# An mLSTM layer with an MLP on one core: a planner's order replaced by a fixed list, a 128-row third K tile, and the norm factor moved to the residual

## The chip, the cores and the metric

The kernel runs on one NeuronCore of a Trainium2 chip. The number that counts is device time in microseconds (us) of one execution, input layouts prepared beforehand on the host. The profile comes from one further execution of the same program on the chip; its times are in us from the first to the last instruction, which the profile calls the span. Engines carry the profile's names: PE is TensorE, PEld its weight loads, DVE is VectorE, ACT is ScalarE, POOL is GpSimd, SP is SyncE, which here only issues DMAs.

## What is computed

Four batches, 8 heads, 768 time steps, head size 40, all in fp32. First a gated recurrence in every head, then layer norm and a two-layer MLP on the 320 joined features:

```python
for t in range(S):
    m_new = np.maximum(f_gate[:, :, t] + m, i_gate[:, :, t])
    f_stab = np.exp(f_gate[:, :, t] + m - m_new)
    i_stab = np.exp(i_gate[:, :, t] - m_new)
    ...
    C = f_stab * C + i_stab * einsum('bhd,bhe->bhde', vt, kt)
    n = f_stab * n + i_stab * kt
    h_tilde = einsum('bhde,bhe->bhd', C, qt)
    denom = np.maximum(np.abs(einsum('bhd,bhd->bh', n, qt)), 1.0)
    y[:, :, t] = sigmoid(o_gate[:, :, t]) * h_tilde / denom
x  = y with the heads joined                    # (4, 768, 320)
xn = (x - mean(x)) / np.sqrt(var(x) + 1e-06) * g_ln
out = x + np.maximum(xn @ w_ch1, 0.0) @ w_ch2   # 320 -> 1280 -> 320
```

(The shapes of f_stab and i_stab are left out in this copy.)

## The kernel before

**Tiling.** Time is cut into 6 chunks of 128 steps. One chunk of one batch is a *step* `st` (24 of them, chunk by chunk, 4 batches in each); two steps are a *pair* `p` (12), and the MLP of one pair's 256 tokens is a *unit* `u` (12).

**A step.** For each head PE multiplies keys and queries into a 128x128 tile `s` (L411). A matrix `w` of decays comes from the gates: the gate rows of the chunk lie in DRAM (`gsc`), a DMA spreads 8 of them, 512 KB, over 128 partitions (`load_G`, L332), POOL cuts the triangle (`select`, L339), ACT takes 8 exponentials with a bias from `ar_sb` (L363). DVE multiplies `s` into `w` (`emit_P`, L418). PE then forms `Y`: the part from earlier chunks out of the state (`emit_inter`, L432, with queries that POOL has scaled by `eg`, L346) and the part within the chunk (`emit_pv`, L481). There is one buffer `Y`, so `emit_inter` of the next step waits until `Y` has been read. The state is updated from L444, L462 and L470.

**The norm.** DVE takes the denominator and its reciprocal (L496, L502, L507), POOL multiplies it into the output gate (`norm_o`, L514: `ogr`), DVE multiplies `Y` by it (L523: `y`, which frees `Y`). Mean and variance come from ACT in half of the steps and from DVE in the others, the root from POOL (L549 to L553: `rstd`), then DVE writes the normalized row twice (L560, and 64 of its columns again, L563). PE turns it (`emit_T`, L578: `xT`), ACT and DVE split it into a high part `xh` with g_ln as a scale (three instructions, L584) and a low part `xl` (L596).

**A unit.** fp32 precision is reached with fp32r operands in high and low parts. `mm1` (L615) adds 8 matmuls of 256 columns into `h` for each block of 128 hidden features; I call these 8 a *batch*; a unit has 10. The 320 features are two K tiles of 128 rows and a third that holds the last 64 features twice (high part in rows 0 to 63, low part in rows 64 to 127). The low half of w1 meets that third tile in its 64 upper rows alone, a matmul of 64 rows:

```python
ops += [(w1l[:, k, cs], XH[:, k]) for k in range(2)]
ops += [(w1l[0:64, 2, cs], XH[0:64, 2])]
```

ACT takes the relu (`hh`, L619), DVE the low part (`hl`, L625), and `mm2` (L639 to L641) adds 6 matmuls of 320 columns for each half of the tokens. DVE adds the residual `y` (L645), SP stores (L649).

**The start.** Weights arrive as 64-bit integers and are taken apart on the chip: one ACT pass, one max pass, three passes on DVE (L681, L685, L689), a high part from ACT (L712), a low part from DVE or POOL (L717); 11 pieces in all. The first three pairs read queries and keys as fp32 with 40 rows; later ones are split and stacked into 120 rows by 6 DMAs in each step (`stack`, L257). For the first 2 steps PE itself makes the decays (`mask_mm`, `sel_mm`, L378 and L389), and 41 matmuls on zeros (`keep_busy`, L373) stand between the others.

**The order.** A planner (`Plan`) hands out tasks by readiness, by assumed durations and by a table of ranks and offsets; each engine then runs its own list strictly in that order. All loads and stores are issued by SP, in one list, and an entry that waits holds up those behind it. In the planner's table an `mm1` batch stands with 0.87 us.

Of the kernel before, what the change touches and what calls it, by code (L numbers as in the profile page):

```python
# [30 lines left out]

TUNE = dict(
    NN=3, k=5, xt=2, yb=4, wb=4, RA=26.71, RB=21.56, f0=18.16, f1=30.7, fd=0.84, ke='aada', ge='dppppp', ns='aaaaadddddaadddadaaddaad', cx='ddpdpdpdpdp', cl='dpddpdpdpdd', nr=-31.54, pr=-13.12, x2=5.36, kd=-11.22, c0=20.24, GP=2, sp=4.1, cst=0.81, og0=2.6, wl0=3.88, wl1=8.52, nt1=8.16, g2=16.0, wu=9, T0=24.67, SL=22.64, EX=6.21, g1=-7.43, p2=0.83, tok1=15.21, s2=6.94, n2=0.0, n3=26.21, og1=29.93, cv=-6.4, cs=2.76, wl=0.34, ws=2.19
)
# [1006 lines left out]
```

## Time and profile before

| | us |
|---|---|
| median of 3 runs (479.43 to 485.68) | 480.65 |
| span of the profiled execution | 477.9 |
| PE busy in it | 440.4 (92%) |
| DVE, ACT, POOL busy | 230.4, 176.2, 159.5 |

The profiled execution's span is 2.75 us under the median; the times count a little work around the span. "Busy" of PE counts matmuls that overlap as one stretch, so it tells when PE had something in flight, not how densely it worked: for that the distance between the starts of matmuls has to be read. [...]

### The profile page before, as it was taken

What the parts mean: (1) busy time and instruction counts of PE and PEld (TensorE: products, weight loads), DVE (VectorE), ACT (ScalarE), POOL (GpSimd) and SP (SyncE); (2) the same over time, 40 slices, a digit from 0 to 9 for tenths busy, and PEclk for the clock granted to TensorE, in tenths of its full rate; (3) what the DMA queues carried; (4) which work ended last, traced back from release to release, by engine and by line L of the source; (5) the groups of instructions that cost most, each with busy time, mean ns of one, the idle gap of its engine ahead of it and who ended that gap; (6) DMA issues with size and microseconds to landing.
All of it is one profiled execution on the core that took longest, in us unless ns stands there. A gap on an engine that the chain in (4) does not pass through costs nothing.

```text
span 477.9 us, 7347 instructions
## 1 busy us (share of the span) xinstructions
PE 440.4 (92%) x2704; PEld 386.5 (81%) x2706; DVE 230.4 (48%) x524; ACT 176.2 (37%) x438; POOL 159.5 (33%) x195
## 2 busy tenths in 40 slices
PE   8999998999789997699998799988979988999996
PEld 4886787889679886688997698977868977989885
DVE  2475869975164752544545325453463443433321
ACT  3356556751151343414443313244243334222200
POOL 1145449661341560613623433252250522100100
PEclk8555779899979999579999859999997998999999
DMA  8935757637845879425776743686465585000000
GB/s 241 291 103 148 233 148 256 163 93 207 190 124 145 235 206 213 122 80 169 194 198 162 183 126 110 161 237 184 130 194 167 132 259 118 1 0 29 0 29 27
DMA packets 52721, 71.82 MB, mean 150 GB/s; under 512 B 3330, under 2 KB 45862, under 8 KB 52686
## 3 DMA queue, kind: packets, MB, share of 16 engines
q1 hardware_dynamic: 52686, 71.36, 54.1%
q8 instruction: 21, 0.34, 0.3%
q14 instruction: 14, 0.11, 0.1%
HBM read 46.83 MB, written 4.12 MB: 107 GB/s over the span
## 4 chain that ended last, share of the span: by engine, by line
PE 61%; DMA 22%; DVE 7%; SPq 3%; POOL 2%; issue 2%; ACT 2%; POOLq 0%; DVEq 0%; ACTq 0%
PE h L615 25%; DMA w<-gsc 8%; PE Y L481 6%; PE o L639 5%; PE s L411 5%; PE o L641 5%; PE o L640 5%; PE kv L444 2%; DMA og<-in_og_dram 2%; DMA raw<-in_qk_dram 2%; DMA ks<-raw 2%; DMA qs<-hi 2%; DMA qs<-raw 2%; SPq L257 2%; DMA eg<-esc 2%
## 5 line engine op out<-in xcount | busy, mean ns | idle before, releaser
L615 PE MATMUL h<-xh,w1h 128*128 128x256 f32 x360 | 91.2, 312 | 0.0
L615 PE MATMUL h<-xh,w1l 128*128 128x256 f32 x360 | 89.4, 327 | 0.0
L639 PE MATMUL o<-w2h,hh 128*128 128x320 f32 x240 | 83.1, 346 | 6.6 <-ACT hh L619 5.4
L619 ACT ACTIVATE hh<-h 128x512 fp32r<-128x512 f32 x60 | 35.6, 594 | 136.0 <-PE h L615 124.4
L641 PE MATMUL o<-w2h,hl 128*128 128x320 f32 x240 | 77.3, 322 | 0.5 <-DVE hl L625 0.5
L640 PE MATMUL o<-w2l,hh 128*128 128x320 f32 x240 | 76.8, 320 | 0.0
L615 PEld LDWEIGHTS h<-xh,w1l 128*128 128x128 f32 x360 | 62.8, 200 | 16.6 <-issue 2.5
L625 DVE SCALAR_TENSOR_TENSOR hl<-h,hh 128x512 fp32r<-128x512 f32 x60 | 41.2, 687 | 63.0 <-ACT hh L619 62.8
L363 ACT ACTIVATE w<-w,ar_sb 128x128 f32<-128x128 f32 x176 | 55.0, 390 | 33.1 <-POOL w L339 32.9
L615 PEld LDWEIGHTS h<-xh,w1h 128*128 128x128 f32 x360 | 64.3, 204 | 0.6
L615 PE MATMUL h<-xl,w1h 128*128 128x256 f32 x240 | 63.6, 348 | 0.0
L481 PEld LDWEIGHTS Y<-tok,w 128*128 128x128 f32 x384 | 55.4, 216 | 1.5 <-POOL rstd L552 1.1
L481 PE MATMUL Y<-tok,w 128*128 128x42 f32 x384 | 53.9, 293 | 0.6 <-ACT xh L584 0.6
L639 PEld LDWEIGHTS o<-w2h,hh 128*128 128x128 f32 x240 | 48.0, 200 | 7.5 <-ACT hh L619 5.8
L615 PEld LDWEIGHTS h<-xl,w1h 128*128 128x128 f32 x240 | 37.9, 199 | 16.4 <-issue 2.2
L641 PEld LDWEIGHTS o<-w2h,hl 128*128 128x128 f32 x240 | 47.6, 198 | 1.5 <-DVE hl L625 1.5
L418 DVE TENSOR_TENSOR w<-s,w 128x512 f32<-128x512 f32 x48 | 33.0, 688 | 31.4 <-PE s L411 26.5
L640 PEld LDWEIGHTS o<-w2l,hh 128*128 128x128 f32 x240 | 47.8, 199 | 0.0
L411 PE MATMUL s<-qs,ks 120*128 120x128 f32 (+1 forms) x240 | 41.0, 305 | 3.9 <-DMA qs<-raw 2.0
L411 PEld LDWEIGHTS s<-qs,ks 120*128 120x128 f32 (+1 forms) x240 | 36.2, 217 | 8.4 <-issue 7.5
L514 POOL TENSOR_TENSOR ogr<-og,rec 128x320 f32<-128x320 f32 x24 | 18.8, 781 | 65.3 <-DVE rec L507 50.1
L248 POOL TENSOR_TENSOR raw<-raw,hi 120x768 f32<-120x768 f32 x18 | 33.0, 1837 | 14.9 <-ACT hi L243 14.9
(91 smaller groups left out, 518.2 us busy)
## 6 DMA issues: line engine op xcount, KB each, us to landing
w<-gsc SPq DMA_DIRECT2D x22, 512.0 KB
tok<-in_tok_dram SPq DMA_DIRECT2D x12, 698.0 KB
raw<-in_qk_dram SPq DMA_DIRECT2D x9, 720.0 KB
ks<-hi SPq DMA_DIRECT2D x36, 180.0 KB
qs<-hi SPq DMA_DIRECT2D x36, 180.0 KB
out_dram<-y SPq DMA_DIRECT2D x24, 160.0 KB
qn<-in_qn_dram SPq DMA_DIRECT2D x10, 360.0 KB
eg<-esc SPq DMA_DIRECT2D x30, 120.0 KB
```

The source lines that it names most:

```text
L248: nc.gpsimd.tensor_tensor(out=raw[:, :, j], in0=raw[:, :, j], in1=hi[:, :, j], op=ALU.subtract)
L363: nc.scalar.activation(out=w[:, h], in_=w[:, h], func=AF.Exp, bias=ar_sb[:, c, 0, hb:hb + 1])
L411: nc.tensor.matmul(ps[:, hh], ks[:, h], qs[:, h], start=True, stop=True)
L418: nc.vector.tensor_tensor(out=w[:, half * 4:half * 4 + 4], in0=s_t.pop((st, half)), in1=w[:, half * 4:half * 4 + 4], op=ALU.mult)
L481: nc.tensor.matmul(Y[:, h * VA:(h + 1) * VA], w[:, h], tok_t[p][:, j, h * VA:(h + 1) * VA], start=(c == 0), stop=(c == 0 or h == H - 1), s ...
L514: nc.gpsimd.tensor_tensor(out=ogr, in0=og_t[c][:, b].rearrange("p (h d) -> p h d", h=H), in1=rec.to_broadcast([128, H, D]), op=ALU.mult,)
L615: nc.tensor.matmul(ps[:, i], a, x, start=(n == 0), stop=(n == len(ops) - 1))
L619: nc.scalar.activation(out=hh, in_=h1_t[p, f], func=AF.Relu)
L625: nc.vector.scalar_tensor_tensor(out=hl.rearrange("p a t -> p (a t)"), in0=ps.rearrange("p a t -> p (a t)"), scalar=0.0, in1=hh.rearrange( ...
L639: nc.tensor.matmul(ps, hh[:, i, sl], w2h[:, ff], start=(ff in (0, 2 * cut)), stop=False)
L640: nc.tensor.matmul(ps, hh[:, i, sl], w2l[:, ff], start=False, stop=False)
L641: nc.tensor.matmul(ps, hl[:, i, sl], w2h[:, ff], start=False, stop=(ff in (2 * cut - 1, KF - 1)))
```

## The change

The planner, its tables and its dummy matmuls are gone. A list of words, `ORDER`, names every piece of work in its order, and a loop calls them:

```diff
-        plan.run()
+        for word in ORDER.split():
+            name, *at = word.split(".")
+            fn = work.get(name) or work[name + "_"]
+            fn(*map(int, at))
```

No word of it is `fill`, the one piece that would issue dummy matmuls. The pieces themselves differ in these places.

**Third K tile.** The last transpose takes features 192 to 319, so that the last 64 land in rows 64 to 127; the low part overwrites rows 0 to 63. The low half of w1 is copied into both halves of its third tile (a fourth copy `cR`), and all 8 matmuls have 128 rows:

```diff
-        for k in range(3):
+        for k in range(2):
             nc.tensor.transpose(ps[:, k], xn[:, k * 128:(k + 1) * 128], id_sb)
+        nc.tensor.transpose(ps[:, 2], xn[:, DM - 128:DM], id_sb)
...
-        ops = [(w1h[:, k, cs], XH[:, k]) for k in range(2)]
-        ops += [(w1l[:, k, cs], XH[:, k]) for k in range(2)]
-        ops += [(w1l[0:64, 2, cs], XH[0:64, 2])]
+        ops = [(w1h[:, k, cs], XH[:, k]) for k in range(3)]
+        ops += [(w1l[:, k, cs], XH[:, k]) for k in range(3)]
         ops += [(w1h[:, k, cs], XL[:, k]) for k in range(2)]
-        ops += [(w1h[:, 2, cs], XH[:, 2])]
```

**Norm.** `norm_o` on POOL is gone. DVE multiplies gate and `Y` at once (`n2`, frees `Y`), then divides, sums and subtracts the mean (`n3`). The variance is taken by ACT beside the path (`sq`), its root by POOL (`np_`), and it is multiplied in only at the residual (`ob`); g_ln is multiplied into w1 when the weights are taken apart:

```diff
+    def n2(st):
+        Y = Y_t.pop(st).rearrange("p (h d) -> p h d", d=VA)
...
+        nc.vector.scalar_tensor_tensor(
+            out=y_t[st].rearrange("p (h d) -> p h d", h=H), in0=og_t[p][:, j].rearrange("p (h d) -> p h d", h=H),
+            scalar=1.0, in1=Y[:, :, 0:D], op0=ALU.add, op1=ALU.mult,
+        )
...
+        nc.vector.reciprocal(out=t1, in_=t1)
+        nc.vector.scalar_tensor_tensor(
+            out=y, in0=y, scalar=1.0, in1=t1.to_broadcast([128, H, D]), op0=ALU.mult, op1=ALU.mult, accum_out=sm
+        )
+        nc.vector.tensor_scalar(out=sm, in0=sm, scalar1=-1.0 / DM, scalar2=None, op0=ALU.mult)
+        xn = xn_p.tile([128, DM], F32, tag="xn", name="xn")
+        nc.vector.tensor_scalar(out=xn, in0=y_t[st], scalar1=sm, scalar2=None, op0=ALU.add)
...
+    def sq(st):
...
+        nc.scalar.activation(out=og_t[p][:, j], in_=xn_t[st], func=AF.Square, accum_out=rs)
...
+        nc.scalar.activation(out=XH_t[p][:, :, j * C:(j + 1) * C], in_=xp_t[st], func=AF.Copy)
...
+            out=y_t[st], in0=m2_t[j], scalar=rs_t.pop(st), in1=y_t[st], op0=ALU.mult, op1=ALU.add
```

**Gate rows.** They lie batch first in DRAM, so that the 8 rows of a step are one run of 4 KB instead of 8 of 512 bytes:

```diff
+            out=w.rearrange("p h t -> p (h t)"),
+            in_=gsc[c].rearrange("(b h) t -> b (h t)", b=B)[b:b + 1].to_broadcast([128, H * C]),
```

The scaled rows `esc` are stored by 5 DMAs in each chunk instead of 2.

**Chunk 0.** All 4 of its steps take their decays from PE (2 before), with `gc` as an operand of 128 rows, zero below row 31; 20 DMAs spread gate rows instead of 22. Only two pairs read fp32 queries and keys, so 20 steps are stacked instead of 18. The gate tile is three half-chunk buffers, `y` has 5 buffers (4), and the low half of w1 comes from DVE always.

**How the lists move.** PE, at a batch of `mm1` in the middle of the program (`h` is its target), before:

```order
L615 MATMUL h<-xh,w1h 128x256 x2
L615 MATMUL h<-xh,w1l 128x256 x3
L615 MATMUL h<-xl,w1h 128x256 x2
L615 MATMUL h<-xh,w1h 128x256
L411 MATMUL s<-qs,ks 128x128 x4
```

and now:

```order
L579 MATMUL h<-xh,w1h 128x256 x3
L579 MATMUL h<-xh,w1l 128x256 x3
L579 MATMUL h<-xl,w1h 128x256 x2
L544 MATMUL xT<-id_sb,xn 128x128 x2
L545 MATMUL xT<-id_sb,xn 128x128
```

The 8 matmuls are the same in number, 3, 3 and 2 instead of 2, 3, 2 and 1; the third `w1l` matmul has 128 rows of operands now, and 64 before.

POOL, over a stretch of about four steps in the middle of the program, before (`ogr` is `norm_o`, `rstd` the root, `qn` scaled queries, `w` the decays, `kp` scaled keys, `raw` low parts of the split):

```order
L339 AFFINE_SELECT w<-w 128x1024
L346 TENSOR_TENSOR qn<-qn,eg 120x3x128
L514 TENSOR_TENSOR ogr<-og,rec 128x320
L346 TENSOR_TENSOR qn<-qn,eg 120x3x128
L339 AFFINE_SELECT w<-w 128x1024
L549 TENSOR_SCALAR rstd<-mv 128x1
L550 TENSOR_TENSOR rstd<-rstd,mh_sb 128x1
L248 TENSOR_TENSOR raw<-raw,hi 120x2x384 x2
L514 TENSOR_TENSOR ogr<-og,rec 128x320
L352 TENSOR_TENSOR kp_140<-tok,ar_sb 128x320
L352 TENSOR_TENSOR kp_141<-tok,ar_sb 128x320
L339 AFFINE_SELECT w<-w 128x1024
```

and now (`rs` is the root):

```order
L415 TENSOR_TENSOR kp_137<-tok,ar_sb 128x320
L352 TENSOR_TENSOR raw<-raw,hi 120x2x384 x2
L532 TENSOR_SCALAR rs<-rs 128x1
L533 TENSOR_TENSOR rs<-rs,mh_sb 128x1
L357 AFFINE_SELECT w<-w 128x1024
L532 TENSOR_SCALAR rs<-rs 128x1
L533 TENSOR_TENSOR rs<-rs,mh_sb 128x1
L357 AFFINE_SELECT w<-w 128x1024
L415 TENSOR_TENSOR kp_138<-tok,ar_sb 128x320
L415 TENSOR_TENSOR kp_137<-tok,ar_sb 128x320
L415 TENSOR_TENSOR kp_138<-tok,ar_sb 128x320
```

`ogr` is gone, and `rs` is read only at the residual; `w`, `raw`, `kp` and `qn` still stand in one list.

SP, at the stores of one unit in the middle of the program (`raw` are queries and keys of a later pair, `w` the decays, `eg` the scaled rows), before:

```order
L649 DMA out_dram<-y 128x320
L297 DMA gsc<-gc_148 32x128
L303 DMA esc<-gg_146 32x128
L304 DMA esc<-gg_146 4x128
L211 DMA raw<-in_qk_dram 120x1536
L221 DMA qn<-in_qn_dram 120x768
L324 DMA eg<-esc 120x1x256 x3
L649 DMA out_dram<-y 128x320
L332 DMA w<-gsc 128x8x128
```

and now:

```order
L196 DMA raw<-in_qk_dram 120x1536
L620 DMA out_dram<-y 128x320
L208 DMA qn<-in_qn_dram 120x768
L255 DMA eg<-esc 120x1x256 x3
L620 DMA out_dram<-y 128x320
L243 DMA w<-gsc 128x1024
```

The two stores stand among the loads as before, the next decays behind the second one.

## Rows read from the trace of the kernel before

**Rows 1.** The page: busy us of each engine, share of the span, instructions.

```profile
PE 440.4 (92%) x2704; PEld 386.5 (81%) x2706; DVE 230.4 (48%) x524; ACT 176.2 (37%) x438; POOL 159.5 (33%) x195
```

**Rows 2.** Stretches: length; busy (count) PE, PEld, DVE, ACT, POOL; clock; DMA share, GB/s.

```profile
0.00:53.00 53.00, 49.31 (x210) 36.45 (x212) 28.48 (x66) 25.62 (x69) 17.52 (x29) 0.65 0.70 207
53.00:95.20 42.20, 40.58 (x226) 35.34 (x225) 34.87 (x63) 25.70 (x61) 27.72 (x26) 0.80 0.65 187
95.20:424.00 328.80, 300.22 (x1947) 270.06 (x1946) 151.54 (x364) 115.31 (x289) 112.01 (x135) 0.92 0.59 158
424.00:477.90 53.90, 50.31 (x328) 44.61 (x326) 15.55 (x34) 9.55 (x21) 2.25 (x5) 1.00 0.05 19
```

**Rows 3.** Order of time, PE, at clock 1.0: start us, length, line, tiles, rows, count.

```profile
432.80 0.40 PE L615 MATMUL h<-xh,w1h 128*128 128x256 f32 x2
433.04 0.70 PE L615 MATMUL h<-xh,w1l 128*128 128x256 f32 x3
433.67 0.50 PE L615 MATMUL h<-xl,w1h 128*128 128x256 f32 x2
434.01 0.28 PE L615 MATMUL h<-xh,w1h 128*128 128x256 f32 x1
434.13 0.31 PE L639 MATMUL o<-w2h,hh 128*128 128x320 f32 x1
```

**Rows 4.** The same at clock 0.5.

```profile
205.88 1.14 PE L615 MATMUL h<-xh,w1l 128*128 128x256 f32 x3
206.95 0.80 PE L615 MATMUL h<-xl,w1h 128*128 128x256 f32 x2
207.54 0.41 PE L615 MATMUL h<-xh,w1h 128*128 128x256 f32 x1
207.75 1.46 PE L444 MATMUL kv<-tok,kp 128*120 128x126 f32 x6
```

**Rows 5.** Groups by shape, weight loads: count, busy us, mean ns, idle us before them.

```profile
L615 PEld LDWEIGHTS h<-xh,w1h 128*128 128x128 f32 x360 | 64.3, 204 | 0.6
...
L615 PEld LDWEIGHTS h<-xh,w1l 128*128 128x128 f32 x240 | 39.7, 203 | 0.0
L615 PEld LDWEIGHTS h<-xl,w1h 128*128 128x128 f32 x240 | 37.9, 199 | 16.4 <-issue 2.2 <-DVE w L418 0.2
L615 PEld LDWEIGHTS h<-xh,w1l 64*128 64x128 f32 x120 | 23.1, 193 | 16.6 <-issue 2.5 <-ACT wt L671 0.2
```

**Rows 6.** What PE waited for: us in total, times, longest us.

```profile
PE Y L432 <- DVE y L523: 12.3, 5, 6.3
PE xT L578 <- DVE xn L560: 6.1, 4, 3.5
PE o L639 <- ACT hh L619: 5.4, 2, 4.7
```

**Rows 7.** Groups, POOL, the gate times the reciprocal.

```profile
L514 POOL TENSOR_TENSOR ogr<-og,rec 128x320 f32<-128x320 f32 x24 | 18.8, 781 | 65.3 <-DVE rec L507 50.1 <-ACT og L232 15.2
```

**Rows 8.** The chain that ended last, 112 to 140 us: start us, us, what.

```profile
117.02 11.90 DMA w<-gsc
...
129.05 1.11 POOL w L339
...
133.37 0.63 PE o L639
```

**Rows 9.** Groups, DVE, 0 to 95.2 us: count, busy us, mean ns.

```profile
L689 DVE SCALAR_TENSOR_TENSOR wraw<-wraw,wt 128x640 int32<-128x640 int32 (+1 forms) x11 | 10.6, 966 | 0.1
L681 DVE TENSOR_SCALAR wt<-wt 128x640 int32<-128x640 int32 (+1 forms) x11 | 9.1, 826 | 0.6 <-POOL wt L676 0.6
L685 DVE SCALAR_TENSOR_TENSOR wt<-wraw,wt 128x640 int32<-128x640 int32 (+1 forms) x11 | 9.0, 814 | 0.0
L418 DVE TENSOR_TENSOR w<-s,w 128x512 f32<-128x512 f32 x11 | 7.5, 685 | 8.3 <-ACT w L402 4.6 <-PE s L411 3.6
```

**Rows 10.** What the DMA queue of SP waited for.

```profile
SPq L649 <- DVE y L645: 97.5, 16, 27.9
```

More of the change, by code (lines that the diff above doesn't have):

```diff
@@ L446, in emit_kv, with kd @@
             )
[L447 to L449 removed]
+        kv_t[st] = ps
+    @piece
+    def kd(st):
         c, b = divmod(st, B)
[L451 to L463 removed]
@@ L465, in emit_state, with st_ @@
-    def emit_state(st):
+        ps = kv_t.pop(st)
+        if c == 0:
+            dst = state[b]
+        else:
+            dst = kv_t[st] = kv_p.tile([120, 3, 126], F32, tag="km", name="km")
+        nc.vector.tensor_tensor(
+            out=dst[:, 0:2], in0=ps[:, 0:2], in1=bd_sb.to_broadcast([120, 2, 126]), op=ALU.mult
+        )
+        nc.vector.tensor_tensor(out=dst[:80, 2, :84], in0=ps[:80, 2, :84], in1=bd_sb[:80, 0, :84], op=ALU.mult)
+    @piece
+    def st_(st):
         b = st % B
@@ L476, in emit_pv, with pv @@
+    def pv(st, half):
         c, b = divmod(st, B)
@@ L546, in norm_p @@
[L546 to L565 removed]
+    @piece
@@ L653, in wload @@
[L653 to L668 removed]
+    keys = ["r"] + [(x, f) for f in range(KF // 2) for x in ("a", "b")]
@@ L669, in conv_a, with wl, cA @@
+    @piece
+    def wl(n):
+        key = keys[n]
+        src, m = (w1r, 640) if n == 0 else (w1a[key[1]], 512) if key[0] == "a" else (w2[key[1]], 640)
+        t = stage_p.tile([128, 640], I64, tag="raw", name="wraw", bufs=BUFS["wraw"])
+        nc.sync.dma_start(out=t[:, :m], in_=src)
+        w_st[n] = t
+    @piece
+    def cA(n):
+        m = 512 if keys[n][0] == "a" else 640
+        raw = w_st.pop(n)[:, :m].bitcast(I32).rearrange("p (n two) -> p n two", two=2)
         lo, hi = raw[:, :, 0], raw[:, :, 1]
-        t = stage_p.tile([128, 640], I32, tag="t", name="wt")[:, :n]
+        t = stage_p.tile([128, 640], I32, tag="t", name="wt")[:, :m]
@@ L934, in consts, with parts @@
-    def consts():
+            w_st[n] = lo.bitcast(F32)
+    def parts(n):
+        key, t = keys[n], w_st[n]
+        if n == 0:
+            for h in range(2):
+                ps, cs = slice(64 * h, 64 * h + 64), slice(640 * h, 640 * h + 640)
+                yield t[ps], w1h[ps, 2, cs], w1l[ps, 2, cs], g_sb[ps, 2:3]
+        elif key[0] == "a":
+            cs = slice(key[1] * 256, (key[1] + 1) * 256)
+            for k in range(2):
+                yield t[:, k * 256:(k + 1) * 256], w1h[:, k, cs], w1l[:, k, cs], g_sb[:, k:k + 1]
+        else:
+            f = 2 * key[1]
+            yield t.rearrange("p (k c) -> p k c", k=2), w2h[:, f:f + 2], w2l[:, f:f + 2], None
@@ new lines, in cH, with cL @@
+    @piece
+    def cH(n):
+        for t, h, _, g in parts(n):
+            nc.scalar.activation(out=h, in_=t, func=AF.Copy, **({} if g is None else dict(scale=g)))
+    @piece
+    def cL(n):
+        for t, h, l, g in parts(n):
+            if g is None:
+                e = nc.gpsimd if CX[n] == "p" else nc.vector
+                e.tensor_tensor(out=l, in0=t, in1=h.bitcast(F32), op=ALU.subtract)
+            else:
+                nc.vector.scalar_tensor_tensor(
+                    out=l, in0=t, scalar=g, in1=h.bitcast(F32), op0=ALU.mult, op1=ALU.subtract
+                )
+        w_st.pop(n)
```

981 lines of the change are left out of this document (343 added, 638 removed).

## The prediction

> **What bounds the kernel now.** I read the page first: PE is busy 92% of the span and no other engine half of it [rows 1]. So the first question is what PE does in that time, not who else is slow. The table of stretches cuts the span at the first `mm1` matmul (53.0 us), at that of the second unit (95.2), at that of the unit before the last (424) and at the end [rows 2]. To 95 us PE runs at a granted clock of 0.65 and 0.80, and from 53 to 95 us DVE is busy 34.9 of 42.2 us: the start belongs to DVE, which takes weights apart. From 95 to 424 us PE has something in flight 300 of 329 us at a mean clock of 0.92; with two levels, 0.5 and 1.0, that is 16% of the time, 53 us, at the lower one. The tail is PE alone at full clock.
>
> Then the distances between starts inside one `mm1` batch [rows 3]. At full clock two `w1h` matmuls take 433.04 - 432.80 = 0.24 us, and the last one 434.13 - 434.01 = 0.12, so 0.12 us each. But the three `w1l` matmuls, of which the third has 64 rows, take 0.63 and the two `xl` behind them 0.34. Five matmuls take 0.97 us where five at the going rate would take 0.60: 0.37 us are lost in a batch. At the lower clock it is 1.07 + 0.59 = 1.66 us against 5 x 0.21 = 1.05 [rows 4]: 0.61 us lost. The weight loads tell where: before loads of 128 rows that follow 128 rows the loader idles 0.0 and 0.6 us in all, before the 120 loads of 64 rows 16.6 us, and before the `xl` loads, the first behind them, 16.4 [rows 5]. The next load does not start early when the number of rows changes.
>
> Last the waits [rows 6]: 12.3 us for `y`, which frees `Y`; 6.1 us for `xn`; 5.4 us for `hh`. Two of these run through POOL: `ogr` stands behind whatever POOL waits for, and it is busy 0.78 us itself [rows 7]. The chain shows such a stop whole: decays `w` issued at 117.0 land 11.9 us later, POOL cuts them, ACT's list stands behind, and PE goes on at 133.4 [rows 8].
>
> **The change part by part**, against this execution's 477.9 us.
>
> *Third K tile.* All 8 matmuls of a batch have 128 rows, so the loader meets no change of rows. 120 batches [rows 5]; about 11 run at the lower clock (the second stretch holds 10 and has 40% of its time there, the third 90 and 16%, and half as many batches pass per us). 109 x 0.37 = 40.3, 11 x 0.61 = 6.7, 47 in all. The ten batches of the first unit hold 4 of it, and they stand beside DVE's work, so I count them at nothing: **-43**, of which 35 fall into the third stretch and 7 into the tail. Bounds: 0 (rival C) and -49, with the first unit's and with 20 batches at the lower clock.
>
> [...]
>
> *Norm.* `Y` comes free after two small DVE passes and one of 320 columns with no trip to POOL or back, and `xT` no longer waits for POOL's root. Of the 12.3 + 6.1 us [rows 6] I take three quarters, **-14**, because what is late behind some of these stops is the same `w`, whose ACT work also stands ahead of `hh` [rows 8]. Bounds -18.4 and 0. On DVE the pass that divides and sums is new, the second writing of 64 columns and the moments go; DVE is busy 151.5 of 328.8 us there [rows 2], which covers a pass a step. POOL loses 18.8 us [rows 7], and ACT three small passes in each step for one.
>
> *Clock.* 53 us at the lower level between 95 and 424 us cost half of what PE worked in them: at most 53/2 = 26, of which the batches' 0.24 us each are counted already. They follow stops of PE: behind that at 133 us a first matmul takes 0.63 us [rows 8] that takes 0.31 at full clock [rows 3]. With most stops shorter and batches without holes in them I take **-10**. Bounds -22 and 0.
>
> *Start.* 41 dummy matmuls go; 32 more real ones (8 heads in 2 steps, two passes each) come, at 0.21 us or less apart [rows 4] 7 us at most, and PE waited on DVE there anyway. DVE was busy 28.5 + 34.9 = 63.4 us to 95.2 [rows 2]. In the new list it must do, before the second unit: 10 pieces of weights with three passes each, 10 x 2.61 = 26 us; 12 products, 12 x 0.69 = 8 [rows 9]; and the rest, which took 63.4 - 28.7 - 7.5 = 27 us before [rows 2, 9]. Some 35 further passes of DVE stand ahead of that place now (masks of the state in two pieces and its first updates, gates of two more chunks, parts of five norms); at half a us each, an estimate between nothing and the 0.69 of a 512-column pass [rows 9], they make it 45. That is 79 in all. It idled 32 us before; some 18 of them are first loads and gates, which stay: 97 against 95.2, **+2**. Bounds -8 and +12, by 10 us less or more of idle time.
>
> *DMA.* The decays' 4 KB runs and two fewer of them ease the queue, 12 more stacking DMAs and 15 more small stores load it; no row prices a packet, so I set these against each other. What counts is the pace: the third stretch moved its bytes at a share of 0.59 [rows 2]. In 328.8 - 35 - 14 - 10 = 270 us the same work needs 0.72, just above the 0.70 that the first 53 us held. I take **+4** for loads that now come late; bounds 0 and +28 (rival A).
>
> *The rest*, at nothing: one `xh` pass for three on ACT and two `xl` for three on DVE lie beside PE's matmuls; a residual pass with a scale is the pass that was there; SP has 5 stores in place of 2 in each chunk, behind which decays wait, in the clear of a chunk's four steps. If PE no longer covers these they cost up to 1 us in each of 12 pairs.
>
> Sum: 477.9 - 43 - 14 - 10 + 2 + 4 = 416.9. The median of the runs stands 2.75 us above this execution's span: **420 us**.
>
> **Rivals.** *A, the DMA pace rules.* PE has less to do, the bytes stay. If the third stretch can hold no more than the 0.65 of the second [rows 2], it takes 328.8 x 0.59 / 0.65 = 298 us, 28 more than the 270 I count; less the 4 already in: 444. For it: decays that took 11.9 us to land [rows 8]. Against: the first stretch's 0.70, and fewer packets. 20%.
>
> *B, nearly all stops go.* Waits -18, clock -22, start -8, no late loads: 477.9 - 43 - 18 - 22 - 8 + 2.75 = 390. Against: loads are still issued from one list. 13%.
>
> *C, the third K tile does not do what it says.* [...] 7%.
>
> *D, slower: SP's fixed list.* Decays for a coming step stand behind the second store of a unit. SP waited 97.5 us for `y` at the stores, once 27.9 [rows 10]; before, a slow PE hid that. If in 9 pairs PE stood for the whole landing, 9 x 11.9 = 107, less the 15 us of stops left in my sum: 420 + 92 = 512. It decides from (490.3 - 420) / 9 = 7.8 us more in each pair. Against: the three largest sums of PE's waits name no DMA [rows 6], so each of those that do is under 5.4 us in all, and three `w` buffers let loads run ahead. 3%.
>
> **Numbers.** My forecast has 57%, with a range of its own from 402 to 436. The range of all reaches down to 390 (half of B) and up to 448 (most of A); left out are C, D and the ends of A and B, about 19%. A measurement of this kernel tells about 2% from no change: under 471.0 is faster, over 490.3 slower. Faster: 57 + 20 + 13 + half of C = 93%; same: the other half of C, 4%; slower: D, 3%.
>
> **What the profile after would show.** `mm1` starts 0.12 us apart through the whole batch and no idle time at any `w1l` load: the first term, and C wrong. PE's waits for `y` and `xn` below 5 us: the second. The clock of the middle at 0.96 or more: the third. The second unit's first matmul between 87 and 107 us: the start. A DMA share of 0.7 in the middle with PE waiting for ACT or POOL that wait for `w` or the stacked tiles: A. SP long in its stores and PE standing just behind: D. I would be wrong most cheaply at the waits, because one late load stops POOL, ACT and PE by turns, and which of them is named changes with the order.

## The result, and the profile after

The changed kernel takes 440.46 us (median of 5 runs, 437.89 to 441.38), the kernel before 483.46 in runs on the same chip (479.43 to 493.98): a ratio of 0.918, 95% interval 0.912 to 0.924. That is faster, as forecast, and 20 us above the forecast of 420. Its profiled execution has a span of 436.1 us. The ratios in this document leave out executions in the slower of the states that the kernels show, so they are not those of the medians.

The page's busy line answers [rows 1], and the table of stretches [rows 2]; it is cut at 53.0 us, at the first `mm1` matmul (78.7), at that of the second unit (110.9), at that of the unit before the last (387.8) and at the end. Columns are as in [rows 2].

```profile
PE 380.0 (87%) x2683; PEld 367.6 (84%) x2683; DVE 227.7 (52%) x550; ACT 158.7 (36%) x385; POOL 143.9 (33%) x172
```

```profile
0.00:53.00 53.00, 34.87 (x149) 30.38 (x149) 25.03 (x60) 20.56 (x48) 17.46 (x26) 0.81 0.75 211
53.00:78.70 25.70, 20.91 (x111) 19.31 (x112) 22.72 (x54) 12.88 (x39) 16.30 (x22) 0.63 0.68 193
78.70:110.90 32.20, 26.55 (x192) 25.76 (x192) 27.77 (x52) 17.25 (x41) 18.83 (x20) 0.92 0.70 199
110.90:387.80 276.90, 252.91 (x1892) 248.14 (x1891) 134.39 (x347) 100.01 (x245) 89.81 (x101) 0.94 0.63 175
387.80:436.10 48.30, 44.71 (x347) 44.01 (x346) 17.80 (x40) 7.97 (x16) 1.48 (x4) 1.00 0.13 44
```

PE was busy 92% and is busy 87%: it has less to do and stands more. The start (up to the second unit) grew from 95.2 to 110.9 us, the third stretch (from there to the unit before the last) fell from 328.8 to 276.9, and the tail from 53.9 to 48.3.

A batch in order of time at full clock, to be read as [rows 3]:

```profile
413.87 0.52 PE L579 MATMUL h<-xh,w1h 128*128 128x256 f32 x3
414.23 0.51 PE L579 MATMUL h<-xh,w1l 128*128 128x256 f32 x3
414.58 0.40 PE L579 MATMUL h<-xl,w1h 128*128 128x256 f32 x2
414.81 0.31 PE L606 MATMUL o<-w2h,hh 128*128 128x320 f32 x1
```

Eight matmuls take 414.81 - 413.87 = 0.94 us; before they took 434.13 - 432.80 = 1.33. The weight loads by shape (as [rows 5]) have lost their two idle groups:

```profile
L579 PEld LDWEIGHTS h<-xh,w1l 128*128 128x128 f32 x360 | 54.8, 202 | 0.0
L579 PEld LDWEIGHTS h<-xl,w1h 128*128 128x128 f32 x240 | 39.4, 202 | 0.0
```

What PE waited for (as [rows 6]: total, times, longest):

```profile
PE kv L442 <- DMA w1l<-w1l: 8.0, 1, 8.0
PE xT L544 <- DVE xn L519: 4.5, 4, 2.7
PE h L579 <- DVE hl L591: 4.3, 1, 4.3
PE s L396 <- DMA qs<-hi: 4.3, 1, 4.3
PE s L396 <- DMA qs<-raw: 4.2, 2, 2.7
...
PE s L396 <- DMA ks<-raw: 2.9, 1, 2.9
```

The 12.3 us for `y` are gone from the head of the list. The first line is named after the wrong thing: `kv` does not read `w1l`. It needs its one PSUM buffer back from DVE, and DVE emptied it only at 39.0 us, behind a pass on a weight piece that landed late; `kv` starts at 39.27 (start us, us, what):

```profile
38.78 0.23 DVE L458 TENSOR_TENSOR state<-kv,bd_sb 80x84 f32<-80x84 f32 x1
```

So this is a stop of the start, for weights. In the third stretch the stacked queries and keys (`qs`, `ks`) lead with 11.4 us together.

**A measure for what follows.** A stretch is made of what PE would need at full clock without a stop, and of the rest. I estimate the first as busy time less length x (1 - clock), from the row of the stretch; the rest is idle time and what the low clock costs. Cut into half microseconds, after shows a granted clock of 1.0 or 0.5 in 853 of 872. Two `xl` matmuls take 414.81 - 414.58 = 0.23 us at 1.0 and 345.57 - 345.14 = 0.43 at 0.5 (from the start of the first to that of the next group); the estimate counts that as twice. The clock has two digits, so this is good to some 2 us. Third stretch of before: 300.2 - 328.8 x 0.08 = 273.9, rest 54.9. Of after: 252.9 - 276.9 x 0.06 = 236.3, rest 40.6.

### The profile page after: what moved, and what is told of

It reads as the page before. It is cut to its first block, busy times and chain, and to the rows that moved or that the text cites. A ratio compares the mean times of both kernels' runs of the same rounds, so it can differ in the third digit from the quotient of the medians.

```text
span 436.1 us, 7316 instructions
## 1 busy us (share of the span) xinstructions
PE 380.0 (87%) x2683; PEld 367.6 (84%) x2683; DVE 227.7 (52%) x550; ACT 158.7 (36%) x385; POOL 143.9 (33%) x172
## 4 chain that ended last, share of the span: by engine, by line
PE 43%; DMA 30%; DVE 10%; SPq 6%; ACT 4%; issue 3%; POOL 3%; POOLq 0%; ACTq 0%; DVEq 0%
PE h L579 15%; DMA og<-in_og_dram 7%; PE Y L479 5%; PE o L608 5%; PE o L606 5%; DMA raw<-in_qk_dram 5%; PE o L607 5%; DMA qs<-hi 4%; DMA eg<-esc 4%; PE s L396 4%; DMA wraw<-in_w1a_dram 3%; DMA qs<-raw 3%; SPq L255 2%; DMA w<-gsc 2%; SPq L233 2%
## 5 line engine op out<-in xcount | busy, mean ns | idle before, releaser
L606 PE MATMUL o<-w2h,hh 128*128 128x320 f32 x240 | 78.8, 329 | 0.0
L608 PE MATMUL o<-w2h,hl 128*128 128x320 f32 x240 | 75.6, 315 | 3.4 <-DVE hl L591 3.4
L579 PE MATMUL h<-xh,w1h 128*128 128x256 f32 x360 | 71.9, 309 | 6.3 <-DVE hl L591 4.3
L579 PE MATMUL h<-xh,w1l 128*128 128x256 f32 x360 | 65.7, 293 | 0.0
L579 PEld LDWEIGHTS h<-xh,w1h 128*128 128x128 f32 x360 | 56.3, 203 | 7.2 <-DVE hl L591 4.5
L368 ACT ACTIVATE w<-w,ar_sb 128x128 f32<-128x128 f32 x160 | 49.7, 390 | 29.2 <-POOL w L357 29.2
L579 PEld LDWEIGHTS h<-xh,w1l 128*128 128x128 f32 x360 | 54.8, 202 | 0.0
L579 PE MATMUL h<-xl,w1h 128*128 128x256 f32 x240 | 50.0, 291 | 0.0
L352 POOL TENSOR_TENSOR raw<-raw,hi 120x768 f32<-120x768 f32 x20 | 36.9, 1853 | 34.4 <-ACT hi L346 34.4
L357 POOL TENSOR_SCALAR_AFFINE_SELECT w<-w 128x1024 f32<-128x1024 f32 x20 | 22.9, 1144 | 49.5 <-DMA w<-gsc 49.5
```

The costliest lines, as they stand in the source:

```text
L352: nc.gpsimd.tensor_tensor(out=raw[:, :, j], in0=raw[:, :, j], in1=t[:, :, j], op=ALU.subtract)
L357: nc.gpsimd.affine_select(out=w, in_=w, pattern=[[0, H], [1, C]], compare_op=ALU.is_ge, fill=NEG, base=0, channel_multiplier=-1)
L368: nc.scalar.activation(out=w[:, h], in_=ps[:, hh], func=AF.Exp, bias=ar_sb[:, c, 0, b * H + h:b * H + h + 1])
L579: nc.tensor.matmul(ps[:, i], a, x, start=(n == 0), stop=(n == len(ops) - 1))
L606: nc.tensor.matmul(ps, t[:, i, sl], w2h[:, ff], start=(ff == 0), stop=False)
L608: nc.tensor.matmul(ps, l[:, i, sl], w2h[:, ff], start=False, stop=(ff == KF - 1))
```

## The experiments

The expectations number the theories. The first is the prediction's: the 64-row matmul costs PE the term of the K tile, and the time follows PE. Theory 2: the start is set by the place of the weight pieces in SP's list. Theory 3: loads set the pace of the third stretch. Theory 4: stores at which SP waits hold up the loads behind them. "After" is the changed kernel, 440.46 us. Experiments 1 to 7 ran on one chip, 8 to 10 on a second, 11 and 12 on a third, each with runs of the kernel before beside it; the ratios are to those.

**1. The 64 rows again, in after.**

```diff
-        ops += [(w1l[:, k, cs], XH[:, k]) for k in range(3)]
+        ops += [(w1l[:, k, cs], XH[:, k]) for k in range(2)]
+        ops += [(w1l[64:128, 2, cs], XH[64:128, 2])]
```

> The changed kernel with the third low matmul of each batch on 64 rows again (rows 64 to 127 of the third tile, the same 64 products; the low-by-low product that the change adds is left out). Theory 1, the hole belongs to the change of rows and lies on the path: 0.37 us a batch at full clock and 0.61 at the lower one come back in 110 batches behind the start, 40 to 48 us slower, about 482 us. Rival, in the new order other waits (late loads, DVE in the start) hide most of it: under 20 us slower, below 460 us. Weight loads should idle again before the 64-row load and the one behind it, 15 us each or more, under both.

Measured: 460.25 us (456.27 to 466.42), ratio to before 0.958 (0.946 to 0.971). The whole hole is back in the weight loads, and the third stretch shows why only 20 us are back in the time:

```profile
L580 PEld LDWEIGHTS h<-xl,w1h 128*128 128x128 f32 x240 | 37.7, 198 | 16.2 <-issue 2.2
L580 PEld LDWEIGHTS h<-xh,w1l 64*128 64x128 f32 x120 | 22.9, 191 | 16.9 <-issue 2.2
```

```profile
118.00:404.20 286.20, 281.61 (x1891) 255.19 (x1890) 135.14 (x347) 99.78 (x245) 89.20 (x101) 0.96 0.60 169
404.20:460.20 56.00, 52.43 (x348) 46.65 (x346) 17.81 (x40) 8.09 (x16) 1.48 (x4) 1.00 0.11 38
```

PE needs 281.6 - 286.2 x 0.04 = 270.2 us there, 33.9 more than in after; the stretch is only 9.3 longer, since the rest fell from 40.6 to 16.0. In the tail, which hardly loads anything (DMA share 0.11), the hole shows whole: 56.0 - 48.3 = 7.7, and 20 batches x 0.39 are 7.8. The start is 118.0 - 110.9 = 7.1 longer in this execution, though the prediction counted the first unit's hole at nothing; in experiment 2, without the hole, it is no shorter (98.1 for 95.2), so this stays open.

**2. The 128 rows alone, in before.**

```diff
-        ops += [(w1l[0:64, 2, cs], XH[0:64, 2])]
+        ops += [(w1l[:, 2, cs], XH[:, 2])]
```

and one more copy of w1's low half. 

> The kernel before with this one part of the change alone: the third low matmul reads all 128 rows (its weights are copied into both halves by one more DMA), in the planner's order as it was. Theory 1, the third K tile is the whole gain and the other parts together come to nothing: 436 to 444 us. Rival, the other parts (norm, gate rows, new order) bring 10 us or more: 451 us or more here. A third way, they cost: below 433 us.

Measured: 462.55 us (457.21 to 466.39), ratio 0.962 (0.949 to 0.976). The third stretch:

```profile
98.10:415.20 317.10, 272.12 (x1946) 264.17 (x1946) 150.85 (x362) 114.11 (x289) 111.12 (x134) 0.90 0.61 163
```

PE's need falls by 273.9 - (272.1 - 317.1 x 0.10) = 33.5 us and the stretch by 11.7: the rest grew from 54.9 to 76.7. So in either kernel the K tile takes some 34 us of work from PE in this stretch, and two thirds of them come back as stops and low clock. The other parts of the change bring a further 22 us, from 462.55 to 440.46.

**3. GpSimd in the path of Y again.** In after, the gate is multiplied by the reciprocal on POOL before `Y` is read:

```diff
+        nc.gpsimd.tensor_tensor(
+            out=o, in0=o, in1=t1.to_broadcast([128, H, D]), op=ALU.mult,
+        )
...
-            scalar=1.0, in1=Y[:, :, 0:D], op0=ALU.add, op1=ALU.mult,
+            scalar=1.0, in1=Y[:, :, 0:D], op0=ALU.mult, op1=ALU.mult, accum_out=sm,
```

> The changed kernel with the gate times the reciprocal on POOL again, in the way of Y (one more POOL pass and one more ACT pass a step or half chunk, one DVE pass of 320 columns less). Theory 1, the norm's way through POOL costs what I took for it, 14 us: 450 to 456 us. Rival, the waits for Y were waits for late loads under another name: within 5 us of the changed kernel, with PE waiting for y a few us and less for the stacked tiles.

Measured: 450.09 us (449.55 to 452.22), ratio 0.941 (0.933 to 0.948): 10 us slower than after. PE's waits and POOL's:

```profile
PE Y L432 <- DVE y L516: 20.7, 9, 5.9
```

```profile
POOL og L507 <- DVE t L499: 86.3, 16, 13.9
```

The wait of [rows 6] is back, nine times, larger than in before.

**4. Gate rows head first, in after.** The decays are read in runs of 512 B for 4 KB, and two stores replace five.

```diff
-            in_=gsc[c].rearrange("(b h) t -> b (h t)", b=B)[b:b + 1].to_broadcast([128, H * C]),
+            out=w, in_=gsc[c:c + 1].rearrange("o (h b) t -> o h b t", b=B)[:, :, b].to_broadcast([128, H, C]),
```

> The changed kernel with gate rows head first again, so that the decays of a step are read in 1024 runs of 512 bytes instead of 128 of 4 KB, and the scaled rows stored by 2 DMAs instead of 5. If packets load the queue (20 x 896 more of them, share of the DMA engines up by 2 or 3 hundredths) and the loads set the pace: 5 to 15 us slower, 445 to 455 us. Rival, loads have slack or the 5 stores cost as much: within 4 us of the changed kernel.

Measured: 439.10 us (437.22 to 440.99), ratio 0.918 (0.908 to 0.928): no difference. The queue itself did change (packets, MB, share of the 16 engines' span; after first):

```profile
q1 hardware_dynamic: 35013, 72.76, 59.2%
q1 hardware_dynamic: 52853, 72.76, 62.7%
```

With the same bytes the packets took 3.5% of 436.1 = 15 us more of the engines' time, and the kernel is no slower. The edit also takes three stores a chunk away, so a small price of the packets could be hidden by that.

**5. Weight pieces first in SP's list.** The words `wl.1` to `wl.3` move ahead in `ORDER`, the decays of step 4 and what hangs on them back:

```diff
-int.0 ini id gin tok.0 nat.0 gl msk.0.0 bd gm.0 og.0 gg.0 wl.0 gate.0 tok.1 gx.0.0 gu.0 gm.1 gg.1 nat.1 S.0.0 sig.0
+int.0 ini id gin tok.0 nat.0 gl msk.0.0 bd gm.0 og.0 gg.0 wl.0 wl.1 gate.0 tok.1 gx.0.0 gu.0 gm.1 gg.1 nat.1 wl.2
```

> The changed kernel with the first three weight pieces loaded ahead of what chunk 1 needs (decays, scaled rows and scaled queries of steps 4 to 7 moved back in SP's list, and with them one POOL cut and two ACT passes of step 4). Theory 2, the start lost its time to weights loaded late (pieces 2 and 3 were issued at 21.8 and 37.1 us, 8.3 and 9.0 in the kernel before): the second unit starts 6 to 12 us before 110.9 us, and the whole is 5 to 12 us faster, 428 to 435 us. Rival, the start is bound by its bytes whatever their order (0.75 of the DMA engines): within 3 us of the changed kernel.

Measured: 437.19 us (434.88 to 439.48). The second unit begins at 107.6, 3.3 us earlier. In after the pieces are issued from 3.7 on, and those that read `in_w1a` from 15.0 (in before from 8.0); ACT waits 16.2 us for the pieces. Here it waits 1.2, and in the same view of before nothing waits for them. From the view of this tile on SP up to 60 us, after first:

```profile
L631 SPq DMA_DIRECT2D wraw<-in_w1a_dram x3: 357/445/2064, 15.0 to 50.0; - x3
...
  ACT wt L640: 16.2, 4
```

```profile
L631 SPq DMA_DIRECT2D wraw<-in_w1a_dram x3: 352/363/425, 4.3 to 49.5; - x3
...
  ACT wt L640: 1.2, 3
```

The wait went, and PE stands once for 8.0 us for the decays that were pushed back:

```profile
PE s L396 <- DVE w L402: 8.0, 1, 8.0
```

Theory 2 accounts for 3 of the start's 16 us, no more: the bytes are the same, and what goes first chose who waits. DVE's idle time up to 53 us stays (28.0 us in after, 28.4 here). For the whole kernel the gain is not clear of the noise: the ranges overlap, and the profiled execution is not shorter (437.7 us, for 436.1).

**6. Fewer bytes.** No token loads for pairs 4 to 11 (these compute with older tiles):

```diff
     def tok_(p):
+        if p > 3:
+            tok_t[p] = tok_t[p - 2]
+            return
```

> The changed kernel without the loads of keys and values for pairs 4 to 11 (8 of 698 KB; it computes these pairs with the tiles of pairs 2 and 3). Theory 3, behind the start the loads set the pace, because the bytes are 5.6 of 73 MB and the third stretch moves 175 GB/s: if all of it were pace, 32 us less; I expect 10 to 25 us faster, 415 to 430 us, with PE's idle time down by as much. Rival, it is the order and the latency of single loads and not their bytes: within 6 us of the changed kernel.

Measured: 421.16 us (420.38 to 427.40). The third stretch:

```profile
111.00:370.30 259.30, 244.07 (x1892) 239.26 (x1891) 133.73 (x347) 99.63 (x245) 90.29 (x101) 0.98 0.58 165
```

No compute engine has less to do (PE's need is 238.9, within 3 us of after), and the stretch is 17.6 us shorter. The rest halves, from 40.6 to 20.4, when 8% of the bytes go, though the queues were busy only 0.63 of the time. Could it be the waits for the token tiles themselves? POOL's waits in the stretch, in after and then here:

```profile
POOL w L357 <- DMA w<-gsc: 36.3, 9, 8.2
POOL kp L415 <- DMA tok<-in_tok_dram: 15.6, 3, 6.5
```

```profile
POOL w L360 <- DMA w<-gsc: 16.4, 5, 5.4
```

The 15.6 us went with the loads, but no token load stands in after's chain of the stretch, and the wait for decays, which are loaded as before, more than halved. SP saves 8 issues of some 0.43 us (the median of the token loads in after), too little. So theory 3 stands: the other loads come earlier when these go. What in the loads sets the pace is open, since experiment 4 added 15 us to the engines' time at no cost.

**7. Stores behind later loads.** Each `out` word moves behind up to three loads; the first of them (words in order, cut):

```diff
-ob.0.0 out.0.0 m2.0.4.1 qk.4 m1.1.3.1
+ob.0.0 m2.0.4.1 qk.4 out.0.0 m1.1.3.1
```

> The changed kernel with every store moved behind up to three later loads in SP's list (where the y buffers allow it). Theory 4, SP's standing at stores (73 us in all, 17 times) delays the loads that PE waits for: 5 to 15 us faster, 425 to 435 us, waits at stores under 40 us. Rival, a load that comes earlier waits for its buffer instead: within 4 us of the changed kernel.

Measured: 474.35 us (471.67 to 477.02), 34 slower. DVE now waits for the row buffers that the stores give back, and PE for DVE:

```profile
DVE y L503 <- DMA out_dram<-y: 46.7, 10, 7.5
```

```profile
PE xT L544 <- DVE xn L519: 27.0, 6, 7.3
PE Y L430 <- DVE t L513: 15.2, 4, 7.4
```

Theory 4 falls in this form: what earlier loads may bring is lost through the buffers. It doesn't show what stores from another queue would do.

**8. Experiments 1 and 6 together**, the sharpest test between theories 1 and 3. 

> The kernel after with two edits at once: the third low matmul on 64 rows again, and no token loads for pairs 4 to 11 (these steps compute with the tiles of pairs 2 and 3, so 5.6 MB are left out). With all loads the 64 rows cost 20 us, of some 43 that TensorE loses in its batches (0.36 us in each of 120). Theory 3 (the loads set the pace of the third stretch, so part of a longer TensorE is hidden behind them): with fewer bytes less is hidden, and the same 64 rows cost 28 to 42 us over the 421 of the kernel with fewer bytes: 449 to 463. Rival (something other than the loads, the order of the engines' work for one, hides the half): 64 rows cost 20 or less here too, 435 to 442.

Measured: 450.03 us (446.08 to 458.37), ratio 0.935 (0.922 to 0.948): 29 over experiment 6, against 20 over after. The profiled execution is the one of 458.37; its start has a granted clock of 0.69 (0.80 in experiment 6), so only its third stretch is used:

```profile
122.60:400.60 278.00, 274.54 (x1892) 248.56 (x1890) 135.28 (x347) 100.09 (x245) 90.04 (x101) 0.99 0.54 151
```

PE needs 271.7, 32.8 more than in experiment 6, and 18.7 of that show in the length, twice the 9.3 of experiment 1. The stretch is nearly all PE's now (rest 6.3). The 20 and the 29 us have overlapping errors and come from two chips; the stretches say it more clearly, with one execution each.

**9. Fewer bytes with nothing left out.** The odd pairs from 3 on read queries and keys with 40 rows, as the first pairs do:

```diff
-st.5 pv.5.0 stk.6 hh.0.2 kd.6
+st.5 pv.5.0 nat.6 hh.0.2 kd.6
...
-    nn = NN
+    nn = NP
```

So for each of their steps; the words `qk`, `hi` and `lo` of these pairs go, and `q0` is laid out for all pairs. 

> The kernel after, nothing left out, with the query and key rows of the odd pairs from 3 to 11 (10 of 24 steps) loaded head by head as 40 rows and multiplied in full fp32, as chunk 0's first pairs are already: of the 73 MB some 11 go (per pair 0.74 MB of raw rows and 2.2 MB of copies, for 0.66), with ScalarE's and GpSimd's work on them. TensorE pays for it: a step's scores took 1.3 us with stacked rows and 3.4 with 40 rows (the latter at a lower clock in part), so 10 to 20 us more. Theory 3 (loads set the third stretch): its idle time falls from 24 towards 12 and its low-clock time from 31 towards 10, worth some 20: 430 to 442 in all. Rival (TensorE's added work counts in full and nothing comes back): 450 to 460.

Measured: 433.41 us (431.02 to 435.44), ratio 0.903 (0.893 to 0.913); 61.8 MB are moved for 73.2. PE's price, by shape (16 matmul records of 40 rows make a step, or 8 of 120):

```profile
L395 PE MATMUL s<-qs,ks 40*128 40x128 f32 x224 | 38.0, 318 | 0.8 <-DMA ks<-in_q_dram 0.8
L395 PE MATMUL s<-qs,ks 120*128 120x128 f32 x80 | 14.0, 304 | 4.2 <-DMA qs<-hi 4.2
```

That is 38.0 / 14 = 2.7 us a step for 1.4, with the start's steps at a lower clock in it; in the third stretch alone it is 19.4 / 8 = 2.4 for 10.5 / 8 = 1.3. It is paid from the stops:

```profile
106.80:378.00 271.20, 258.76 (x1956) 250.38 (x1955) 139.50 (x347) 94.46 (x241) 75.81 (x93) 0.96 0.50 143
```

PE needs 247.9 there, 11.6 more than in after, and the rest fell from 40.6 to 23.3. This run alone does not show that it is the bytes: the edit also takes the split of these pairs from ACT and POOL (POOL 89.8 to 75.8 us in the stretch) and 4 DMAs a step from SP. Only experiment 6 takes bytes and little else.

**10. The same in all pairs**, with the edit of 9 for pairs 2 to 11. 

> As the run with 40-row scores in the odd pairs, but in all pairs (20 more steps, some 23 MB fewer than the kernel after). Theory 3: what the loads hold is used up by the first half of it, and the rest is TensorE's: 438 to 455, above the run with the odd pairs alone, with TensorE idle under 12 us in the third stretch. Rival (the added TensorE work counts in full): 465 to 480. If the loads are worth more than thought, this one is under the run with odd pairs.

Measured: 432.66 us (426.62 to 434.05); 50.3 MB. The middle:

```profile
106.80:378.00 271.20, 268.14 (x2016) 257.77 (x2015) 131.08 (x347) 88.76 (x237) 61.15 (x85) 0.97 0.36 111
```

Idle time is 3.1 us: almost no time is left in stops and PE's own work sets the length. 11.5 MB fewer than in experiment 9 give nothing that stands clear of the spread.

**11. Decays of chunk 0 by DMA.** Words `G.0` to `G.3` and POOL's mask `sel` stand in place of `msk` and `gx`; for step 0:

```diff
-gate.0 tok.1 gx.0.0 gu.0
+gate.0 tok.1 gst.0 G.0 gu.0
...
-wl.1 cX.0 gx.0.1 cT.0.0
+wl.1 cX.0 sel.0 cT.0.0
```

In steps 1 to 3 the mask came between the two halves of the heads, so the first half goes without it: the work is the same, but ACT's second half waits for POOL. 

> The kernel after with one part undone: the gate rows of chunk 0 (steps 0 to 3) come as four broadcast transfers of 0.5 MB again and GpSimd masks them, where TensorE makes rows and mask in 19.5 us of matmuls. If the bytes set the length of the start (2 MB more at the 200 GB/s that the start moves are 10 us): its 110.9 us become 115 to 124, and the whole 444 to 454. Rival (TensorE's 19.5 us of rows in a start where TensorE is the slow engine at half clock set it): 100 to 108 us and 428 to 438. Third: neither is on the path, 439 to 442.

Measured: 448.86 us (445.52 to 451.09), ratio 0.930 (0.921 to 0.940); second unit at 123.7, 12.8 later. That is what the bytes would do; but SP waits for the gate rows' own store and for a free `w`:

```profile
SPq L242 <- PE Y L478: 8.1, 1, 8.1
SPq L242 <- DMA gsc<-gc: 5.4, 1, 5.4
```

13.5 us of the list standing still are as good an explanation. It shows that TensorE's rows cost less here than these transfers, not why.

**12. A version that beats both.** The edit of 9 for pairs 3, 5, 7 and 9, on top of the order of 5. 

> A version to beat both kernels: 40-row scores in full fp32 in pairs 3, 5, 7 and 9 (not in 11, whose steps lie near the tail, where the queues are half idle: the run with all odd pairs had a tail 3 us longer), and the weight pieces ahead of the later loads in the start as in the run with the weights first. If the gains add: 433 less 3 and less 3, 425 to 431. If the start's gain is given back as waits for the displaced gate rows, as it was in part there: 431 to 436.

Measured: **426.24 us** (422.86 to 431.37), ratio 0.882 (0.874 to 0.891), 14 under after.

```profile
107.20:377.00 269.80, 258.93 (x1955) 250.47 (x1954) 135.56 (x347) 95.97 (x242) 80.04 (x95) 0.96 0.52 148
377.00:425.30 48.30, 44.70 (x348) 43.98 (x346) 17.80 (x40) 7.97 (x16) 1.48 (x4) 0.99 0.14 45
```

Start 3.7 us shorter and third stretch 7.1; PE's need grew to 248.1, the rest fell to 21.7. Its profiled execution ran 427.05, against 437.89 for that of after.

## Why the prediction held, and the step that failed

440.46 us lie within the wide range, 390 to 448, and outside the forecast's own, 402 to 436. Against the profiled span the forecast was 416.9 and came to 436.1, 19.2 us short. By stretches: start 97.2 forecast, 110.9 measured; third 273.8 and 276.9; tail 46.9 and 48.3; the last 1 us is the forecast's rounding.

**Start: failed, 13.7 of the 19.2.** The prediction said "97 against 95.2, **+2**", with bounds -8 and +12; it was +15.7, outside them. DVE's work was sized well: 25.0 + 22.7 + 27.8 = 75.5 us for 79. What failed is "It idled 32 us before; some 18 of them are first loads and gates, which stay": it idled 110.9 - 75.5 = 35.4. The growth of the start is 12.1 us of DVE work and 3.6 of idle time, where the prediction let 14 of its 16 us of new work fall into idle time. 28.0 of the 35.4 lie in the first 53 us (24.5 in before). Two of DVE's waits in the start stand behind weight pieces:

```profile
DVE wt L653 <- POOL wt L647: 8.7, 1, 8.7
DVE wt L647 <- ACT wt L640: 5.3, 2, 2.7
```

I took idle time for something that more work fills, and the new order has loads in it. The chain of the start (start us, us, what):

```profile
22.93 14.17 DMA og<-in_og_dram
37.13 11.14 DMA wraw<-in_w1a_dram
48.30 0.67 ACT wt L640
48.99 0.43 DVE wt L647
```

Two landings, one behind the other, make 25 us of it, at a DMA share of 0.75. Experiment 5 takes 3.3 us back by order, experiment 9 4.1 with fewer bytes (experiment 12 has both, and 3.7 in all). With the pieces first these waits of DVE fall from 14.0 to 2.3 us, but 10.2 come for the displaced decays. So what holds the idle time, the bytes or the order of all loads together, is not settled: experiment 11, which was to speak on bytes here, has two explanations.

**Third K tile: the mechanism right, the size right in PE's time, not in the kernel's.** The hole is the change of rows: it went in after, came back in experiment 1, and went alone in experiment 2. The 35 us forecast for the third stretch are 33.9, 33.5 and 32.8 by the measure above, and the tail's 7 are 7.7. But of that stretch's 34 only 9 to 12 shorten the kernel. The `w1l` and `xl` loads, of full rows behind full rows, idle 0.0 us in after; those on both sides of the 64 rows idle 16.9 and 16.2 in experiment 1. At full clock a change of rows and its return cost a batch 0.39 us (1.33 against 0.94). Why a load behind another number of rows starts late is not shown.

**Waits and clock: right in direction, twice as large, and hidden by the first term.** The forecast was 14 + 10, less 4 for late loads, 20 in all. With the 64 rows in both (before against experiment 1) stops and low clock fall from 54.9 to 16.0, by 39; with 128 rows in both (experiment 2 against after) from 76.7 to 40.6, by 36. From 54.9 to 40.6, where both parts act, 14 are left of it. So the third stretch came out 3 us from the forecast by two errors that cancel, which is luck: the K tile counted whole, the others at half. The sum of terms was built as if stops and work were independent. They are not: when PE gets faster, more of the time goes into stops (experiments 1 and 2), and fewer bytes let more of PE's saving through (experiment 8). The norm is a part of the 39 (experiment 3: 10 us of the whole). The gate rows' order is none (experiment 4). What the fixed order itself brings was not taken apart. That the low clock follows stops, as the prediction has it, after shows too: in its third stretch the clock falls to 0.5 six times, each less than 5 us behind the beginning of a stop of PE of 1.5 to 4.3 us. Of the signs that the prediction named, the clock of the middle reached 0.94, not 0.96, and the second unit began at 110.9, not by 107; `xn` stands under 5 us and `y` below the rows shown.

**Rival A** gave 444, near the measured time, for a wrong reason: it let the third stretch stop at a share of 0.65 and take 298 us, and the excess sits in the start. But its cause, loads as the pace, is what the third stretch has (experiments 6, 8, 10), at a share of 0.63. Its sum went wrong because it kept the engines' time: length x share was 194 us before and is 174 now. **B** did not come: its start and its vanishing stops are both missing. **C**, that the hole stays although all 8 matmuls have 128 rows, is refuted by experiments 1 and 2 (33.9 and 33.5 us of PE's time). **D**: SP waited 73.2 us for `y` at the stores (97.5 before, [rows 10]), the longest 16.9, but PE's waits above don't name the decays that stand behind them.

## What to carry to other kernels

Before a stretch's saving is counted in full, ask what the waiting parts do when the engine gets faster: with loads in the stretch about a third of PE's saving came through here (9.3 of 33.9 us, 11.7 of 33.5), in the tail with hardly any loads all of it (7.7 of 7.8). Idle time in a start is not spare time until what ends it is named; read the landings first (here two made 25 us of it). And where stops are due to loads, a slower form of work that moves fewer bytes can be the faster one (experiment 9, 433.41 us for 440.46).

## What had not been expected

- A mean DMA share of 0.63 in the third stretch is no sign that loads have slack: 5.6 of 73 MB fewer gave 19 us.
- 40-row scores in fp32 cost PE 2.4 us a step for 1.3 in the third stretch, and the kernel got faster (433.4, and 426.2 with the better order).
- Decays read in runs of 4 KB or of 512 B made no difference (440.5 and 439.1; five stores for two go with the former), with 17,840 packets more for the latter.
- SP's 73 us at stores could not be had back by issuing loads first: the held stores cost 34 us, through five row buffers.
